# Stores begun by GpSimd, operand rows asked for two at a time, and loads moved in the plan of a fused attention and two-layer kernel

## The chip, the cores and the metric

One core of a Trainium2 chip runs the whole program. The metric is the device time of one execution in microseconds (us). The kernel before took 1796.57 us (median of 3 runs, 1793.56 to 1800.48).

## What is computed

```python
# q, k, v: (8, 8, 576, 64)   batch, heads, sequence, head size
q_s = softmax(q, axis=-1);  k_s = softmax(k, axis=2)          # 1e-9 added to each sum
kv  = einsum('bhsd,bhse->bhde', k_s, v)
x   = einsum('bhsd,bhde->bhse', q_s, kv) -> (4608, 512)
x   = (silu(x @ w_gate) * (x @ w_val)) @ w_out                # 512 -> 1536 -> 512, float64 weights
out = elu(x @ w_in) @ w_out2                                  # 512 -> 2048 -> 512, float64 weights
```

Every matrix product is made from three float32r matmuls of high and low parts (hi x hi, hi x lo, lo x hi), so each operand is split by a ScalarE copy (hi) and a VectorE subtraction (lo).

## The kernel before, in words

The 4608 rows are nine blocks of 512. The order of the work is written out by hand: every engine has its own queue in program order, and an instruction that must wait stops everything behind it on its engine. A DMA is such an instruction too, on the queue of the engine that begins it. SyncE (SP) begins nearly all of them, ScalarE the stores of converted weights and of partial outputs, GpSimd none.

**First stage** (`run_a`, about 28 to 550 us). For block i there are six f (128 of the first 768 hidden columns), each with sub-steps s = 0 (gate projection), 1 (value projection) and 2 (product with `w_out` for the f before). A sub-step written (f, s) below also carries attention work for block t = i + 1, named in `PLAN` (line 1778; `PLAN0` and `PLAN1` serve i = 0 and 1). For t >= 3 the normalised q is transposed through DRAM: `qturn` transposes on VectorE, `qout` (line 548) stores to `dq`, `qin` (line 555) loads pairs into two `qT` buffers, `xT` (line 596) multiplies them with kv. `in0` and `in1` are the two halves of `qin`; `xT0` uses in0's pairs and `xT2` in1's, so in1's load overwrites buffers that xT0's matmuls (line 638) read. `load_k`, `load_v` and `load_q` fetch the next block's inputs, `kmax` and `qmax` are their first readers on VectorE.

Alongside, `conv` (line 278) turns float64 weights into float32 in four steps: load, scale, bits, split. From weight chunk 21 on, the result goes to DRAM: single chunks by one store (line 244), pairs of chunks by `sums_out` (line 266), in which GpSimd makes four sums and ScalarE begins four stores two sub-steps later. Four `cd` buffers and one `st` buffer hold what is being stored. `store_x` (line 653) lets GpSimd add x's hi and lo parts; SP stores the rows two sub-steps later. `defer(age, fn)` puts fn off to a later call of `aged()`, and there is one such call for each sub-step or tick.

**Second stage** (`unit_b`, `single_b`, about 575 to 1009 us). The other 768 hidden columns, for units of two blocks, with products made from seven instead of eight sub-products (`product`, line 1093, with operands M1 to M7). Each step calls `tick` six times. A tick does at most one operation of `xd_tick` (line 1039), which prepares the operands of the last layer: `xd_rows` asks for rows of the block outputs `ys` (four loads, two tiles), `xd_open` makes the sums on GpSimd, and then in each tick one operand is split: a ScalarE copy into a fresh slot `xst` (line 1059) and, in the next tick, the VectorE subtraction (line 1033) and a store to `xd`. The slot goes back (`drop`) as the store is begun. `slot4` hands out the slot that has been vacant longest from one pool of 25, which `g` tiles, operands and weights share. In the first unit the weight sums `s` are split in place (`part_split`, line 1067) on ScalarE and VectorE.

**Third stage** (`run_2`, from about 1009 us): the last layer in the same manner. `load_s` (line 1338) loads a step's weight sums and puts their split in a list; `hold` counts the steps that it waits there, and `run_splits` emits it in the middle of a step. For the first two steps `load_s(0)` and `load_s(1)` are called in `single_b` (line 1721).

Of the kernel before, what the change touches and what calls it, by code (L numbers as in the profile page):

```python
# [17 lines left out]
def kernel(  # L18
# [103 lines left out]
    def drop(n):  # L122
        vacant.append(n)
# [103 lines left out]
    def conv_split(eng):  # L227
        n = stage["split"]
        if n >= stage["bits"]:
            return  # L230
        kind, f = chunks[n][0]
        if n >= NA1 and kind in "giv":
            if stage["bits"] < n + 2:
                return
            d1, d2 = ds[n].bitcast(FP32), ds[n + 1].bitcast(FP32)
            sums_out(sd[f // 2] if kind == "i" else sf[kind, (f - HALF) // 2], d1, d2)
            stage["split"] += 2
            ds.pop(n)
            ds.pop(n + 1)
            return  # L240
        if n >= NA1:
            stage["split"] += 1
            d = ds.pop(n).bitcast(FP32)
            defer(1, lambda: nc.scalar.dma_start(out=wd[f] if kind == "p" else wb[f], in_=d))
            return
        if not room(("w",)):
            return
        at, w = slot4(("w",), [128, 2, 512], "w")
        stage["split"] += 1
        df = ds.pop(n).bitcast(FP32)  # L250
        nc.scalar.activation(out=w[:, 0, :], in_=df, func=ACTF.Copy)
        eng.tensor_tensor(w[:, 1, :], df, w[:, 0, :].bitcast(FP32), op=ALU.subtract)  # L252
        W[chunks[n][0]] = w
        wslot[chunks[n][0]] = at
# [11 lines left out]
    def sums_out(dst, d1, d2):  # L266
        st = sums(d1, d2)
        flat = lambda t: t.rearrange("p a n -> p (a n)")

        def store():  # L270
            nc.scalar.dma_start(out=dst[0][:, 0], in_=d1[:, 0:256])
            nc.scalar.dma_start(out=flat(dst[1][:, 0:2]), in_=d2)
            nc.scalar.dma_start(out=flat(dst[0][:, 1:4]), in_=flat(st[:, 0:3]))
            nc.scalar.dma_start(out=dst[1][:, 2], in_=st[:, 3])

        defer(2, store)

# [375 lines left out]
    def store_x(t, n):  # L653
        if n == 0:
            x32[t] = ev_p.tile([128, KD, TB], FP32, tag="ev", name="ev")
        x, ns = x_t["a", t], slice(2 * n, 2 * n + 2)
        for c in range(2 * n, 2 * n + 2):
            nc.gpsimd.tensor_tensor(
                x32[t][:, c], x[:, c, 0, :].bitcast(FP32), x[:, c, 1, :].bitcast(FP32),
                op=ALU.add,  # L660
            )
        defer(2, lambda: nc.sync.dma_start(out=xs[t][:, ns], in_=x32[t][:, ns]))

    def first_block():
        kt = at1.tile([128, H, 4, D], FP32, tag="k", name="k")
# [201 lines left out]
    def emit_B(ph, i, f):  # L867
        if f == 0:
            acc_tiles((ph, i))
        at, gt = G.pop((ph, i, f))  # L870
        w = W["o", f]
        last = f == HALF - 1
        for c in range(KD):
            cs = slice(c * 128, (c + 1) * 128)
            mm3(acc[ph, i][c], (w[:, 0, cs], w[:, 1, cs]), (gt[:, 0, :], gt[:, 1, :]),
                f == 0, last)
        drop(at)
        if i == NB - 1:
            drop(wslot.pop(("o", f)))
        if last:  # L880
            ev = ev_p.tile([128, KD, TB], FP32, tag="ev", name="ev")
            for c in range(KD):
                nc.scalar.activation(out=ev[:, c, :], in_=acc[ph, i][c], func=ACTF.Copy)
            nc.scalar.dma_start(out=yps[i], in_=ev)


    yp_t = {}
# [111 lines left out]

    def xd_rows(k):  # L1000
        m, c = divmod(k, 2)
        tags, r = [], []
        for n in range(2):
            at, t = slot4(ANY, [128, 2, TB], "yr", FP32)
            tags.append(at)
            for e in range(2):
                nc.sync.dma_start(out=t[:, e], in_=ys[2 * m + e][:, c + 2 * n])
                r.append(t[:, e])
        xd_r[k] = [0, tags, r]

    def xd_open(k):
        m, c = divmod(k, 2)
# [16 lines left out]
    def xd_lo():  # L1029
        if xd_st["lo"]:  # L1030
            op, src, at, d = xd_st["lo"]
            m, c = xd_st["cur"][0:2]
            nc.vector.tensor_tensor(d[:, 1, :], src, d[:, 0, :].bitcast(FP32), op=ALU.subtract)
            defer(1, lambda: (
                nc.sync.dma_start(out=xd[m][PROD[op]][:, c], in_=d.bitcast(FP32)), drop(at)
            ))
            xd_st["lo"] = None

    def xd_tick(ready):
        k, n = xd_st["k"], xd_st["rows"]  # L1040
        for e in xd_r.values():
            e[0] += 1
        if n < min(6, 2 * ready, k + 2) and room(ANY) >= (4 if n == k else 8):
            xd_rows(n)
            xd_st["rows"] += 1
        if xd_st["cur"] is None:
            if k not in xd_r or xd_r[k][0] < 5:
                return
            xd_open(k)
        xd_lo()  # L1050
        ops = xd_st["cur"][3]
        if not ops:
            for at in xd_st["cur"][2]:
                drop(at)
            xd_st.update(cur=None, k=k + 1)
            return
        op, src, pre = ops.pop(0)
        at, d = slot4(ANY, [128, 2, TB], "xst")
        nc.scalar.activation(out=d[:, 0, :], in_=src, func=ACTF.Copy)
        pre()  # L1060
        xd_st["lo"] = (op, src, at, d)
# [2 lines left out]

    splits, split_now = [], []

    def part_split(hi, lo, age=0):
        nc.scalar.activation(out=hi, in_=lo.bitcast(FP32), func=ACTF.Copy)
        defer(age, lambda: nc.vector.tensor_tensor(  # L1069
            lo, lo.bitcast(FP32), hi.bitcast(FP32), op=ALU.subtract  # L1070
        ))

# [337 lines left out]
    def load_sb(key, parts=(0, 1), n=None, first=False):  # L1410
        for part in parts:
            at = n
            if n is None:
                at = ring[part] % 2
                ring[part] += 1
            t = s_tile(at, part)
            SW.setdefault(key, [None, None])[part] = t
            if not first:
                nc.sync.dma_start(out=t.bitcast(FP32), in_=sb[key][part])
                continue  # L1420
            nc.sync.dma_start(out=t[:, :, 1, :].bitcast(FP32), in_=sf[key][part])
            splits.append([0, lambda age, t=t, part=part: (
                part_split(t[:, :, 0, :], t[:, :, 1, :], age),
                defer(2, lambda: nc.sync.dma_start(out=sb[key][part], in_=t.bitcast(FP32))),
            )])

# [273 lines left out]
    def single_b(u, carry):  # L1700
        NG1 = HALF // 2
        nxt = units[0]
        for g in range(NG1):
            if g == 0:
                mid = carry
                for key in (("g", 1), ("v", 1)):
                    load_sb(key, n=2 if key[0] == "g" else 3)
            else:
                mid = [lambda f=HALF + 2 * g - 2 + e: b_D(u[0], f) for e in range(2)]
            if g == 1:  # L1710
                load_yp(u[0])
            if g == 1:
                x_small(nxt, X_MID[0:2], ANY)
            step_s(u, g, mid, lambda: (aged(), xd_st["k"] < 6 and xd_tick(3)), g == NG1 - 1)
            if g == 0:
                load_sb(("g", 2), n=0)
                load_sb(("v", 2), n=1)
                X[nxt] = ({}, [])
                x_big(nxt, X_HEAD)
            if g == 1:  # L1720
                load_s(0)
                load_s(1)
                x_small(nxt, X_MID[2:], ANY)
        while xd_st["k"] < 6 or later:
            aged()
            if xd_st["k"] < 6:
                xd_tick(3)
        for tag in X.pop(u)[1]:
            drop(tag)
        x_big(nxt, X_LAST)  # L1730
        for f in range(4):
            load_p(f, hold=1 + f // 2)
        carry = [lambda f=f: b_D(u[0], f) for f in (F1 - 2, F1 - 1)]
        carry.append(lambda: (load_s(2), load_s(3, 1), None)[2])
        return carry
# [12 lines left out]
    def side_last(ff, s):  # L1748
# [36 lines left out]
    }  # L1785
    PLAN0 = {
# [15 lines left out]
    def steps(i):  # L1802
# [3 lines left out]
        if t < B:  # L1806
# [7 lines left out]
            else:  # L1814
                st["kturnt"] = lambda: kturn(t)
                st["ks0"] = lambda: ks(t, (0, 1), nc.vector)
                st["ks1"] = lambda: (ks(t, (2, 3, 4), nc.vector), u < B and load_k(u))
            st["load_v"] = lambda: load_v(t)
            if i == 0:
                st["load_k2"] = lambda: load_k(u)  # L1820
# [208 lines left out]
```

## Time and profile before

| | |
|---|---|
| median of 3 runs | 1796.57 us |
| profiled execution: its own time, its span | 1795.31 us, 1793.2 us |
| TensorE matmuls busy | 1682.0 us (94%) |
| VectorE / ScalarE / GpSimd busy | 66% / 45% / 13% |
| granted TensorE clock, mean | 0.976 of full speed |
| DMA moved | 351.95 MB, mean 196 GB/s |

PE stands for TensorE's matmuls, DVE for VectorE, ACT for ScalarE, POOL for GpSimd, SPq and ACTq for the DMA instructions on an engine's queue. A busy PE is not PE at its peak: the time that counts is where it stands still, and the stretch after that in which its clock is granted at half. What ended the chain of work is 73% PE, 9% DMA, 8% DVE, 5% ACT.

### The profile page before, as it was taken

The numbers are of one execution on the slowest core, as the hardware profiler recorded it, in microseconds if no ns is written. First come the engines' busy times: TensorE is split into PE (matmuls) and PEld (weight loads), VectorE is DVE, ScalarE is ACT, GpSimd is POOL, SyncE is SP. The second block draws the span as 40 slices with busy tenths as digits, with TensorE's granted clock in tenths as the row PEclk, the third lists the DMA queues.
The fourth block names the chain that finished last, engine by engine and source line by source line (L and its number), as shares of the span: only waits on it lengthen the run. The fifth ranks groups of instructions, "written<-read, shape, count | busy, mean of one in ns | idle before, by whom it ended". The sixth has DMA issues, their size and how long they took to land.

```text
span 1793.2 us, 22155 instructions
## 1 busy us (share of the span) xinstructions
PE 1682.0 (94%) x8228; PEld 1375.0 (77%) x8228; DVE 1186.3 (66%) x1800; ACT 801.8 (45%) x1339; POOL 233.8 (13%) x196
## 2 busy tenths in 40 slices
PE   6899998889998999998989689999999999999999
PEld 4577777667877788787878568888889888888887
DVE  7858787677756766666756376657674767465574
ACT  4645244334433432323323265656464656355453
POOL 3611121222104204032120000000000000000000
PEclk9999998899999999999999899999999999999999
DMA  9475876695675757587686926272613453352511
GB/s 283 114 181 162 244 231 217 197 267 196 207 246 220 248 221 268 213 302 272 238 304 254 400 71 242 76 270 94 246 67 113 142 198 115 143 184 75 211 47 71
DMA packets 186860, 351.95 MB, mean 196 GB/s; under 512 B 49921, under 2 KB 121857, under 8 KB 172801
## 3 DMA queue, kind: packets, MB, share of 16 engines
q1 hardware_dynamic: 174224, 322.49, 53.2%
q10 hardware_dynamic: 12528, 28.05, 4.2%
q8 instruction: 64, 1.05, 0.2%
q14 instruction: 44, 0.35, 0.1%
HBM read 234.36 MB, written 116.14 MB: 195 GB/s over the span
## 4 chain that ended last, share of the span: by engine, by line
PE 73%; DMA 9%; DVE 8%; ACT 5%; issue 2%; SPq 2%; POOL 2%; ACTq 0%; DVEq 0%; POOLq 0%
PE p L1104 27%; PE y L810 11%; PE y L809 10%; PE y L808 10%; PE a L827 4%; PE a L828 4%; PE a L831 4%; DMA xd<-xst 2%; DVE u L1228 1%; DMA qT<-dq 1%; PE t L638 1%; ACT th L1117 1%; ACT e L1118 1%; DMA s<-sd 1%; PE t L480 1%
## 5 line engine op out<-in xcount | busy, mean ns | idle before, releaser
L1104 PE MATMUL p<-xp,s 128*128 128x512 f32 x1344 | 325.4, 396 | 37.2 <-DVE u L1228 20.4
L1228 DVE TENSOR_TENSOR u<-u,p 128x512 f32<-128x512 f32 x315 | 215.7, 685 | 218.0 <-PE p L1104 203.5
L1104 PEld LDWEIGHTS p<-xp,s 128*128 128x128 f32 x1344 | 255.6, 191 | 94.8 <-DVE u L1228 24.2
L1104 PE MATMUL p<-xs,s 128*128 128x512 f32 (+1 forms) x1260 | 274.4, 372 | 3.1 <-ACT u L1248 3.1
L1104 PEld LDWEIGHTS p<-xs,s 128*128 128x128 f32 x1260 | 224.1, 191 | 45.0 <-ACT u L1248 3.7
L809 PE MATMUL y<-w,g 128*128 128x512 f32 x576 | 225.7, 392 | 4.2 <-DVE w L1069 4.2
L808 PE MATMUL y<-w,g 128*128 128x512 f32 x576 | 225.4, 391 | 1.7 <-ACT g L1143 1.3
L810 PE MATMUL y<-w,g 128*128 128x512 f32 x576 | 226.0, 392 | 0.6
L827 PE MATMUL a<-x,w 128*128 128x512 f32 x424 | 171.1, 403 | 4.5 <-DVE th L858 2.7
L828 PE MATMUL a<-x,w 128*128 128x512 f32 x424 | 167.6, 395 | 0.0
L1123 DVE SCALAR_TENSOR_TENSOR th<-e,th 128x512 f32<-128x512 f32 x144 | 99.2, 689 | 101.9 <-ACT e L1118 100.5
L1116 ACT ACTIVATE e<-u 128x512 f32<-128x512 f32 x108 | 67.7, 627 | 156.3 <-DVE u L1228 156.3
L809 PEld LDWEIGHTS y<-w,g 128*128 128x128 f32 x576 | 108.8, 189 | 27.4 <-DVE w L1069 4.9
L810 PEld LDWEIGHTS y<-w,g 128*128 128x128 f32 x576 | 108.8, 189 | 26.5 <-DVE g L1152 4.0
L808 PEld LDWEIGHTS y<-w,g 128*128 128x128 f32 x576 | 108.9, 189 | 24.8 <-ACT g L1143 1.7
L1152 DVE TENSOR_TENSOR g<-th,g 128x512 fp32r<-128x512 f32 (+1 forms) x160 | 99.9, 634 | 37.7 <-ACT g L1143 35.3
L1143 ACT ACTIVATE g<-th 128x512 fp32r<-128x512 f32 (+1 forms) x160 | 91.3, 580 | 67.7 <-DVE th L1129 67.7
L831 PE MATMUL a<-x,w 128*128 128x512 f32 x424 | 114.4, 392 | 0.6 <-POOL w L252 0.6
L827 PEld LDWEIGHTS a<-x,w 128*128 128x128 f32 x424 | 81.1, 191 | 29.9 <-issue 7.5
L831 PEld LDWEIGHTS a<-x,w 128*128 128x128 f32 x424 | 80.1, 189 | 17.9 <-POOL w L252 1.1
L828 PEld LDWEIGHTS a<-x,w 128*128 128x128 f32 x424 | 81.2, 191 | 16.3
L1117 ACT ACTIVATE th<-e 128x512 f32<-128x512 f32 x144 | 91.1, 633 | 4.6
(204 smaller groups left out, 2638.8 us busy)
## 6 DMA issues: line engine op xcount, KB each, us to landing
xp<-xd SPq DMA_DIRECT2D x32, 1024.0 KB, 10.1
xs<-xd SPq DMA_DIRECT2D x51, 512.0 KB, 7.2
xd<-xst SPq DMA_DIRECT2D x42, 512.0 KB, 9.4
raw<-in_moe_w_out SPq DMA_DIRECT2D x26, 512.0 KB, 5.0
s<-sbg SPq DMA_DIRECT2D x12, 1024.0 KB, 6.5
s<-sbv SPq DMA_DIRECT2D x12, 1024.0 KB, 8.8
yp<-ev ACTq DMA_DIRECT2D x9, 1024.0 KB, 4.5
xs<-ev SPq DMA_DIRECT2D x18, 512.0 KB, 5.1
```

The lines of the kernel that those rows point to most:

```text
L808: nc.tensor.matmul(out=ps, lhsT=wh, rhs=xh, start=first, stop=False)
L809: nc.tensor.matmul(out=ps, lhsT=wh, rhs=xl, start=False, stop=False)
L810: nc.tensor.matmul(out=ps, lhsT=wl, rhs=xh, start=False, stop=last)
L827: nc.tensor.matmul(out=ps, lhsT=wh, rhs=x[:, c, 0, :], start=(c == 0), stop=False)
L828: nc.tensor.matmul(out=ps, lhsT=wh, rhs=x[:, c, 1, :], start=False, stop=False)
L831: nc.tensor.matmul(out=ps, lhsT=wl, rhs=x[:, c, 0, :], start=False, stop=(c == KD - 1))
L1104: nc.tensor.matmul(out=out_, lhsT=w, rhs=x, start=first and (q, c, k) == (0, 0, 0), stop=(c, k) == (1, 2), skip_group_check=True,)
L1117: nc.scalar.activation(out=t, in_=e, func=ACTF.Tanh, scale=-0.5)
L1123: nc.vector.scalar_tensor_tensor(out=t, in0=e, scalar=1.0, in1=t, op0=ALU.add, op1=ALU.mult)
L1143: nc.scalar.activation(out=gt[:, 0, at:at + n], in_=t[:, q * n:(q + 1) * n], func=ACTF.Copy)
L1152: nc.vector.tensor_tensor(gt[:, 1, at:at + n], t[:, q * n:(q + 1) * n], gt[:, 0, at:at + n].bitcast(FP32), op=ALU.subtract,)
L1228: nc.vector.tensor_tensor(o, a, b, op=ALU.add)
```

## The change

Six edits. (1) The stores of converted weights, of their sums and of x's rows are begun by GpSimd; x's rows without the delay of two sub-steps. (2) The store of the partial output `yps` is begun by SP at the next `aged()` instead of by ScalarE. (3) `xd_rows` asks for one tile (two loads) in a tick, and a set opens four ticks after its second tile; an `xst` slot goes back two ticks after its store is begun, and no operand is started while fewer than three slots are vacant. (4) Part 0 of the first unit's weight sums is subtracted by GpSimd. (5) The split of the last layer's second step waits one step more. (6) In `PLAN`, in1 goes from (4, 0) to (3, 2), load_q from (3, 0) to (4, 0), load_k from (1, 0) to (2, 0), kspread from (4, 2) to (5, 1), qmax0 from (4, 2) to (5, 1).

```diff
@@ conv_split
-            defer(1, lambda: nc.scalar.dma_start(out=wd[f] if kind == "p" else wb[f], in_=d))
+            defer(1, lambda: nc.gpsimd.dma_start(out=wd[f] if kind == "p" else wb[f], in_=d))
@@ sums_out, store()
-            nc.scalar.dma_start(out=dst[0][:, 0], in_=d1[:, 0:256])
...
+            nc.gpsimd.dma_start(out=dst[0][:, 0], in_=d1[:, 0:256])
+            nc.gpsimd.dma_start(out=flat(dst[1][:, 0:2]), in_=d2)
+            nc.gpsimd.dma_start(out=flat(dst[0][:, 1:4]), in_=flat(st[:, 0:3]))
+            nc.gpsimd.dma_start(out=dst[1][:, 2], in_=st[:, 3])
@@ store_x
-        defer(2, lambda: nc.sync.dma_start(out=xs[t][:, ns], in_=x32[t][:, ns]))
+        nc.gpsimd.dma_start(out=xs[t][:, ns], in_=x32[t][:, ns])
@@ emit_B
-            nc.scalar.dma_start(out=yps[i], in_=ev)
+            defer(0, lambda: nc.sync.dma_start(out=yps[i], in_=ev))
@@ xd_rows
-        tags, r = [], []
-        for n in range(2):
-            at, t = slot4(ANY, [128, 2, TB], "yr", FP32)
-            tags.append(at)
-            for e in range(2):
-                nc.sync.dma_start(out=t[:, e], in_=ys[2 * m + e][:, c + 2 * n])
-                r.append(t[:, e])
+        tags, r = xd_r.get(k, (0, [], []))[1:]
+        n = len(tags)
+        at, t = slot4(ANY, [128, 2, TB], "yr", FP32)
+        tags.append(at)
+        for e in range(2):
+            nc.sync.dma_start(out=t[:, e], in_=ys[2 * m + e][:, c + 2 * n])
+            r.append(t[:, e])
         xd_r[k] = [0, tags, r]
+        return n == 1
@@ xd_lo
-                nc.sync.dma_start(out=xd[m][PROD[op]][:, c], in_=d.bitcast(FP32)), drop(at)
+                nc.sync.dma_start(out=xd[m][PROD[op]][:, c], in_=d.bitcast(FP32)),
+                defer(2, lambda: drop(at)),
@@ xd_tick
-            xd_rows(n)
-            xd_st["rows"] += 1
+            xd_st["rows"] += xd_rows(n)
...
-            if k not in xd_r or xd_r[k][0] < 5:
+            if k not in xd_r or len(xd_r[k][1]) < 2 or xd_r[k][0] < 4:
                 return
...
+        if room(ANY) < 3:
+            return
         op, src, pre = ops.pop(0)
@@ part_split, load_sb
-    def part_split(hi, lo, age=0):
+    def part_split(hi, lo, age=0, eng=None):
...
-                part_split(t[:, :, 0, :], t[:, :, 1, :], age),
+                part_split(t[:, :, 0, :], t[:, :, 1, :], age, nc.vector if part else nc.gpsimd),
@@ single_b
-                load_s(1)
+                load_s(1, 1)
@@ PLAN, steps
-        "in0": (2, 1), "load_q": (3, 0), "in1": (4, 0), "kspread": (4, 2),
-        "xT0": (3, 2), "xT1": (3, 2), "kturn": (4, 0), "xT2": (5, 0), "xT3": (5, 0),
-        "qmax0": (4, 2), "qmax1": (5, 2),
+        "in0": (2, 1), "load_k": (2, 0), "load_q": (4, 0), "kspread": (5, 1),
+        "xT0": (3, 2), "xT1": (3, 2), "in1": (3, 2), "kturn": (4, 0), "xT2": (5, 0), "xT3": (5, 0),
+        "qmax0": (5, 1), "qmax1": (5, 2),
...
-                st["ks1"] = lambda: (ks(t, (2, 3, 4), nc.vector), u < B and load_k(u))
+                st["ks1"] = lambda: ks(t, (2, 3, 4), nc.vector)
+                if u < B:
+                    st["load_k"] = lambda: load_k(u)
```

## Rows read from the trace of the kernel before

**Rows 1.** The page's first part: busy us (share of the span) x instructions.
```profile
PE 1682.0 (94%) x8228; PEld 1375.0 (77%) x8228; DVE 1186.3 (66%) x1800; ACT 801.8 (45%) x1339; POOL 233.8 (13%) x196
```
**Rows 2.** Waits of PE, whole span: us in total, times, longest us.
```profile
PE t L638 <- DMA qT<-dq: 29.3, 4, 9.4
PE p L1104 <- DVE u L1228: 20.4, 7, 5.7
PE p L1104 <- DVE s L1069: 10.3, 1, 10.3
...
PE p L1104 <- ACT s L1068: 6.4, 1, 6.4
```
**Rows 3.** Waits of PE between 700 and 930 us, same columns.
```profile
PE p L1104 <- DVE u L1228: 14.4, 3, 5.7
```
**Rows 4.** Timeline of PE at stalls: start us, duration us, work, [idle before <- releaser].
```profile
275.00 0.66 PE L638 MATMUL t<-qT,bd 64*64 64x256 f32 x1 [8.34 <-DMA qT<-dq]
...
405.38 0.87 PE L638 MATMUL t<-qT,bd 64*64 64x384 f32 x1 [9.44 <-DMA qT<-dq]
...
822.78 1.65 PE L1104 MATMUL p<-xp,s 128*128 128x512 f32 x3 [5.71 <-DVE u L1228]
...
1026.79 4.18 PE L1104 MATMUL p<-xp,s 128*128 128x512 f32 x10 [10.30 <-DVE s L1069]
```
**Rows 5.** Windows behind two stalls: stretch, length, busy by engine, granted clock, DMA.
```profile
275.00:279.40 4.40, 4.40 (x21) 2.85 (x22) 1.23 (x2) 1.08 (x2) 2.24 (x4) 0.51 0.49 153
822.80:828.90 6.10, 6.10 (x14) 4.77 (x15) 3.26 (x5) 1.64 (x3) 0.00 (x0) 0.50 0.87 357
```
**Rows 6.** Timeline of SP's DMA issues in one block of the first stage.
```profile
232.01 0.37 SPq L340 DMA_DIRECT2D k<-in_k  x1
...
245.63 0.82 SPq L558 DMA_DIRECT2D qT<-dq  x2
...
246.97 7.90 SPq L352 DMA_DIRECT2D vtile<-in_v  x5
...
256.14 2.13 SPq L550 DMA_DIRECT2D dq<-qn  x4
259.58 6.28 SPq L367 DMA_DIRECT2D q<-in_q  x4
265.90 2.49 SPq L377 DMA_DIRECT2D q<-in_q  x4
...
269.43 1.02 SPq L558 DMA_DIRECT2D qT<-dq  x2
```
**Rows 7.** Timeline of SP two blocks later.
```profile
386.75 2.84 SPq L550 DMA_DIRECT2D dq<-qn  x4
```
**Rows 8.** Tile view of `dq`: stores to it and loads from it together.
```profile
DMA to landing us min/median/max: 2.6/3.9/7.2
```
**Rows 9.** Tile view of `qT`: its loads alone.
```profile
DMA to landing us min/median/max: 2.6/3.4/6.1
```
**Rows 10.** Window of one block: length, busy PE, PEld, DVE, ACT, POOL, clock, DMA.
```profile
238.22:303.10 64.88, 56.54 (x330) 45.20 (x332) 47.95 (x75) 26.72 (x37) 11.18 (x12) 0.92 0.74 229
```
**Rows 11.** Timeline of ACT at the second and third stage's stalls.
```profile
820.77 1.15 ACT L1059 ACTIVATE xst<-yr 128x512 fp32r<-128x512 f32 x2 [4.68 <-DMA xd<-xst]
...
1014.16 1.97 ACT L1068 ACTIVATE s<-s 128x1024 fp32r<-128x1024 f32 x2 [17.01 <-DMA s<-sd]
1016.79 1.96 ACT L1068 ACTIVATE s<-s 128x1024 fp32r<-128x1024 f32 x2 [0.66 <-DMA s<-sd]
```
**Rows 12.** Timeline of POOL and DVE in the first unit of the second stage.
```profile
595.60 13.67 POOL L1370 TENSOR_TENSOR v<-v 128x512 f32<-128x512 f32 x8 [31.31 <-DMA v<-xs]
...
595.17 3.18 DVE L1069 TENSOR_TENSOR s<-s 128x1024 fp32r<-128x1024 f32 x2
598.27 1.78 DVE L1469 TENSOR_TENSOR th<-th,u 128x512 f32<-128x512 f32 x1
599.97 0.67 DVE L1469 TENSOR_TENSOR th<-th,p 128x512 f32<-128x512 f32 x1
```

More of the change, by code (lines that the diff above doesn't have):

```diff
@@ L270, in store @@
         def store():
-            nc.scalar.dma_start(out=dst[0][:, 0], in_=d1[:, 0:256])
-            nc.scalar.dma_start(out=flat(dst[1][:, 0:2]), in_=d2)
-            nc.scalar.dma_start(out=flat(dst[0][:, 1:4]), in_=flat(st[:, 0:3]))
-            nc.scalar.dma_start(out=dst[1][:, 2], in_=st[:, 3])
+            nc.gpsimd.dma_start(out=dst[0][:, 0], in_=d1[:, 0:256])
+            nc.gpsimd.dma_start(out=flat(dst[1][:, 0:2]), in_=d2)
+            nc.gpsimd.dma_start(out=flat(dst[0][:, 1:4]), in_=flat(st[:, 0:3]))
+            nc.gpsimd.dma_start(out=dst[1][:, 2], in_=st[:, 3])
         defer(2, store)
@@ L1065 @@
     splits, split_now = [], []
-    def part_split(hi, lo, age=0):
+    def part_split(hi, lo, age=0, eng=None):
         nc.scalar.activation(out=hi, in_=lo.bitcast(FP32), func=ACTF.Copy)
-        defer(age, lambda: nc.vector.tensor_tensor(
+        defer(age, lambda: (eng or nc.vector).tensor_tensor(
             lo, lo.bitcast(FP32), hi.bitcast(FP32), op=ALU.subtract
```

## The prediction, written before the changed kernel was run

> **What bounds the kernel now.** I read the busy shares first: TensorE works 94% of the span [rows 1], so only what is left of it, and stretches at half clock, can be won. The view that decides is therefore the list of TensorE's waits [rows 2]. It has four waits for `qT<-dq`, 29.3 us together, in the first stage; waits for VectorE's line 1228, of which three with 14.4 us lie in the second stage [rows 3]; and two at the start of the last layer, 6.4 and 10.3 us, for the splits of the weight sums `s`. The timeline then shows each of them as one gap [rows 4], and the windows behind a gap show a second price: the granted clock is 0.51 for 4.4 us after the first-stage gap at 275 us and 0.50 for 6.1 us after the one at 822.8 us [rows 5]. That is the lower of the two levels (1.2 of 2.4 GHz), it falls while TensorE stands idle, and work at half speed costs 2.2 and 3.0 us in these two places. The rest of the span has no gap of this size that the diff touches, so I cost the change gap by gap.
>
> **The change, part by part.** The sum is made against the profiled execution, 1795.31 us (span 1793.2), which lies 1.3 us below the median of the runs, 1796.57.
>
> *First-stage loads (edit 6).* Today SP begins, in order, v (246.97 to 254.87), the `dq` stores of the second half (256.14 to 258.27), load_q (259.58 to 268.39, so 6.28 + 2.49 us of issue), and only then in1 at 269.43 [rows 6]. TensorE stands from 275.00 - 8.34 = 266.66 on [rows 4]. So it is the queue order and not the data that makes in1 late. With the new plan in1 stands ahead of load_q. It can't start before the `dq` stores have landed: 258.27 + 3.9 (median, [rows 8]) = 262.2; and it lands 3.4 us later [rows 9], at 265.6. Needed: 266.66. In the block of the longest gap the stores are issued by 386.75 + 2.84 = 389.59 [rows 7]; plus 7.3 makes 396.9, against 405.38 - 9.44 = 395.94 needed, so about 1 us of the gap stays. Moving load_k from (1, 0) to (2, 0) works against this: its 1.1 MB, asked for at 232.01 today [rows 6], would go out at about 242, between the first `dq` stores and in0. SP has free time there (it waits for the `dq` landing until 245.63), so the issue is covered; its bytes at the block's mean of 229 GB/s [rows 10] are 5 us of transfer. They push v and the `dq` stores back by between 0 (the same bytes leave the stretch just ahead, so the backlog there is shorter) and 5 us. I take 1 us, near the first end, because the queue stands idle for lack of data there. Behind in1, load_q is the one that is late next: 8.77 us of issue from about 262 to 271, and qmax0 moves to (5, 1), which VectorE reaches near 270. It waits 1 to 3 us there and the value projection's product waits behind it; TensorE needs that product's bank only two sub-steps later, so I cost 0 to 1.5 us per block and take 0.7. The whole budget is 29.3 us of gaps and 4 x 2.2 us of half clock, 38 us (the clock price of one gap taken for all four). What stays: about 1 + 1 us late landing in two blocks and 4 x 0.7, together 5. **Gain 33 us**, bounds 10 (k's 5 us and a `dq` landing at its maximum of 7.2 us hit every block) and 38.
>
> *Room for the faster step.* A block takes 64.88 us with 8.34 + 2.2 of it lost, so about 54 us without, and VectorE is busy for 47.95 us of it [rows 10]: 6 us of slack are left, which matters for the first rival.
>
> *Stores begun by GpSimd, and `yps` by SP (edits 1, 2).* No row shows a DMA that GpSimd begins. Per block there are about 12 to 14 such stores from `conv` (a pair of chunks gives 4, a single one 1) and 2 of x's rows, so 15. Bounds for one: nothing for anybody else, or, if GpSimd's work for it disturbs VectorE as its arithmetic does, the whole lost time of such a meeting, 1.78 - 0.67 = 1.1 us of VectorE [rows 12]. GpSimd itself is busy for 11.18 of 64.88 us [rows 10], so even at 1.3 us each (20 us) it has the time. I take the value near nothing, since the nearest thing of the same kind, SP's DMA issues at 0.4 us apiece [rows 6], hides in the 6 us of slack (15 x 0.4). ScalarE loses these issues, which gains nothing, as it is busy for 26.72 us of a block [rows 10]. The queue that these stores are moved behind is GpSimd's own, where `store_x` waits for the `yps` landing; stores queued behind it hold `cd` buffers longer, and the one place where VectorE would feel that is the end of the conversion, near 540 us, by 0 to 4 us. There the subtraction of two part-0 sums leaves VectorE as well (edit 4). I set this against that and count 0.
>
> *Operand slots (edit 3).* At 820.77 ScalarE has waited 4.68 us to write a slot whose store has not left yet [rows 11]; VectorE's subtraction and the additions of line 1228 stand behind it, and TensorE loses 5.71 us [rows 4] and 3.0 us of clock [rows 5]. The slot had been handed back when its store was begun. Returned two ticks later and with three slots kept vacant, the next user gets one that has been still for longer; with too few slots it skips the tick instead of stopping ScalarE. Three such gaps are 14.4 us [rows 3], with clock 14.4 + 3 x 3.0 = 23. What is late next: the operations skipped fall into later ticks, at worst into the closing loop of `single_b`, and the wait for the rows themselves remains. **Gain 19 us**, bounds 5 and 23.
>
> *Second step's split (edit 5).* ScalarE waits for the sums of the first step until 1014.16 and goes on with those of the second, 0.66 + 1.96 us until 1018.75, with the last step's gate work and the first split's subtraction behind it [rows 11]; TensorE's 10.30 us end with that [rows 4]. Holding the second split takes 2.6 us off this chain. It comes back inside the next step, where it may delay something by up to 2 us. **Gain 2.5 us**, bounds 0 and 4.
>
> *Subtraction on GpSimd (edit 4).* Near 600 us VectorE's two subtractions take 3.18 us beside GpSimd's sums [rows 12], and one of them goes. **Gain 1.5 us**, bounds -2 (GpSimd's sums, and so the contention, last longer) and 2.
>
> Sum: 33 + 19 + 2.5 + 1.5 = 56 us. 1795.3 - 56 = 1739, on the median's scale 1740.6; with half of the small later prices that I set to nothing I say **1742 us**. Its own range, from the bounds of the two large terms: 1728 to 1762.
>
> **The rivals.**
> (a) *VectorE pays for GpSimd's DMAs* (slower). If each of the 15 stores of a block costs VectorE c us, a block can't be shorter than 47.95 + 15c. Up to c = 0.4 nothing happens; at c = 1.1 the first stage gains nothing; from about c = 1.5 the loss in four blocks (15 x 0.4 x 4 = 24) outweighs edits 3 to 5 (23). At c = 1.78, a whole contended operation, a block takes 74.7 us, 4 x 9.8 = 39 more, less 23: 1812 us. For it: VectorE's operations do stretch beside GpSimd's arithmetic [rows 12]. Against: beginning a DMA is not arithmetic on 512 columns.
> The Trainium skill ("SBUF — State Buffer", section "Who interferes with whom") says that a VectorE instruction with two SBUF inputs contends with a GpSimd instruction that reads SBUF and not with one that only writes, and infers that making DMA descriptors needs the writing side. The first half agrees with the 1.78 against 0.67 us; no run so far shows the second. By that rule c is near nothing and the forecast stands; it is one reason why I give this rival little.
> (b) *in1 is still late.* k's bytes and the `dq` landing push it back by 4 to 5 us in each block, so half of the first stage's 33 us stays: 1742 + 17 = 1759. For: the second block worked out above already misses by 1 us. Against: load_q's 8.77 us of issue certainly leave the way.
> (c) *The operand waits move instead of going* (the pool of 25 runs short, rows or `g` tiles wait in turn): 19 us stay, 1761. For: stores begun late share the same transfers.
> (d) *Both (b) and (c)*: 1742 + 17 + 19 = 1778.
> (e) *Nothing changes that can be measured*, because the gaps close into others as long: 1790 to 1797.
>
> **How the numbers follow.** Forecast 0.54, (a) 0.10, (b) 0.15, (c) 0.09, (d) 0.05, (e) 0.07. Differences under 0.5% (9 us) are about what a measurement of this kernel can't tell from no change. Faster by more than that: 0.54 + 0.15 + 0.09 + 0.05 = 0.83; within: 0.07; slower: 0.10. For the range I leave out the slower case and most of (e) above, and let the low end reach to both large gains at their upper bounds with a few us of the rest: 1724 to 1788.
>
> **What would show it.** In the trace after, the four waits of line 638 for `qT<-dq` are gone or under 2 us each, in1's issue stands ahead of load_q's, and a block of the first stage takes 54 to 56 us. The three waits of line 1228 between 700 and 930 us are gone, ScalarE's line 1059 no longer waits for `xd<-xst`, and no window behind them shows the clock at 0.5. At the start of the last layer ScalarE goes from the first pair of line 1068 straight to the gate work. The prediction is wrong if VectorE's mean for lines 212 to 219 or 858 rises well above the 0.67 us of an undisturbed operation [rows 12] in the first stage, if its waits for `q<-in_q` grow beyond the two sub-steps and TensorE waits for line 858, or if the operands pile up behind the last step of `single_b`.

## The result, and the profile after

The changed kernel takes **1766.16 us** (median of 1762.41 to 1769.02), against 1796.28 in the same runs: ratio 0.9829, 95% interval 0.98 to 0.9858. That is 30 us faster; the forecast was 54 us faster (1742, own range 1728 to 1762, wide range 1724 to 1788). The direction held and the size did not. The profiled execution took 1764.12 us, its span is 1762.4. Of all executions reported here one, of `k_early`, took 4188.05 us; it is in no ratio and in no median below.

First the page's busy shares of the changed kernel, to be read against [rows 1]:

```profile
PE 1679.9 (95%) x8228; PEld 1371.1 (78%) x8228; DVE 1188.9 (67%) x1794; ACT 799.4 (45%) x1339; POOL 299.7 (17%) x298
```

GpSimd has 102 instructions and 66 us more: a DMA that it begins stands in the profile as an instruction. VectorE has as much work as before. Next TensorE's waits over the whole span of the changed kernel, columns as in [rows 2]:

```profile
PE p L1107 <- DVE u L1231: 9.5, 6, 3.7
PE y L809 <- DVE g L846: 9.2, 4, 4.7
...
PE p L1107 <- DVE s L1072: 7.7, 1, 7.7
PE t L638 <- DMA qT<-dq: 6.4, 5, 2.5
PE p L1107 <- ACT s L1071: 5.7, 1, 5.7
PE c L638 <- DVE cd L219: 4.6, 4, 1.4
```

The three waits that the change was costed by have shrunk: `qT<-dq` from 29.3 to 6.4 us, line 1228 (now 1231) from 20.4 to 9.5, line 1069 (now 1072) from 10.3 to 7.7. Beside them the wait for line 846 has grown, from 5.1 us before, and that for line 219 is new; both lines are VectorE's. The windows (columns as in [rows 5]) say where the gain came in. Between the first products of line 480 (`vtile` by `ke`) in the fourth and the last of the eight blocks that have them, before:

```profile
177.60:433.10 255.50, 226.15 (x1314) 180.81 (x1314) 194.07 (x295) 100.95 (x141) 61.11 (x61) 0.93 0.74 225
```

and after:

```profile
177.90:419.50 241.60, 228.47 (x1313) 179.72 (x1312) 196.12 (x290) 99.77 (x140) 92.77 (x118) 0.97 0.83 240
```

These four blocks, for which the forecast had 33 us, gained 13.9; one takes 60.4 us in the mean, where 54 to 56 was forecast. TensorE's idle time in them fell by 16.2 us (29.4 to 13.1) and its busy time rose by 2.3. What the clock costs there (busy time times the share of the clock that was not granted, summed over windows of 1 us) is 6.4 us, against 8.3 before: of the 8.8 us that the budget had for it, about 2 came back. From there to the second stage's first product it lost 2.7 (142.8 to 145.5); the second stage's units up to the first `xa` product gained 16.2 (386.0 to 369.8); the rest gained 3.7 (831.3 to 827.6). The timeline of TensorE after the change, at its stalls:

```profile
254.31 0.61 PE L638 MATMUL t<-qT,bd 64*64 64x256 f32 x2 [1.44 <-DMA qT<-dq]
256.30 0.68 PE L638 MATMUL c<-qT,bd 64*64 64x256 f32 x1 [1.38 <-DVE cd L219]
...
328.70 0.72 PE L638 MATMUL t<-qT,bd 64*64 64x320 f32 x2 [0.88 <-DMA qT<-dq]
...
391.74 0.50 PE L638 MATMUL t<-qT,bd 64*64 64x384 f32 x1 [2.50 <-DMA qT<-dq]
...
560.12 0.80 PE L809 MATMUL y<-g,w 128*128 128x512 f32 x1 [4.73 <-DVE g L846]
...
870.78 1.66 PE L1107 MATMUL p<-xp,s 128*128 128x512 f32 x6 [2.27 <-DVE u L1231]
...
996.32 2.07 PE L1107 MATMUL p<-xp,s 128*128 128x512 f32 x4 [7.68 <-DVE s L1072]
```

The stall at 996.32 answers to that of 10.30 us in [rows 4]. The one at 870.78 is one of two that are left between 700 and 930 us (the other, of 1.93 us, stands before 776.86); neither is at the place of one of the three before. In the block that had the 8.34 us there are now two gaps of 1.4, and the clock is paid again: the window right behind them shows 0.50, the lower of the two levels, as in [rows 5].

```profile
258.00:262.00 4.00, 4.00 (x12) 3.02 (x10) 3.66 (x6) 1.36 (x3) 4.00 (x7) 0.50 1.06 274
```

Why a gap is left, SP's timeline of that block tells (compare [rows 6]):

```profile
238.32 3.20 SPq L550 DMA_DIRECT2D dq<-qn  x4
241.57 0.47 SPq L340 DMA_DIRECT2D k<-in_k  x1
...
246.76 1.33 SPq L558 DMA_DIRECT2D qT<-dq  x2
...
258.06 2.23 SPq L550 DMA_DIRECT2D dq<-qn  x4
...
264.09 1.16 SPq L558 DMA_DIRECT2D qT<-dq  x2
...
265.81 1.90 SPq L367 DMA_DIRECT2D q<-in_q  x4
```

in1 is ahead of load_q, as planned. The late load of this block is now **in0**, asked for at 246.76 and needed at 254.31 - 1.44 = 252.87, and k has been put just in front of it. In the two blocks behind it in1 is late as well, at 328.70 and 330.61 and at 391.74. Of the 6.4 us in the list, in0 has 2.3 and in1 4.2. k's own landing has grown, by the issue view (KB, median us to landing; 178 to 410 us), and VectorE waits for it at `kmax0`, where it did not wait before; for load_q it waits 8.4 us in three blocks at `qmax0` (1 to 3 us a block were forecast), less than the 16.7 us of before:

```profile
k<-in_k SPq DMA_DIRECT2D x4, 1024.0 KB, 11.5
```

```profile
DVE km L389 <- DMA k<-in_k: 8.6, 4, 3.6
DVE qr L503 <- DMA q<-in_q: 8.4, 3, 3.2
```

### The profile page after: what moved, and what is told of

It is laid out like the page before. It is cut to its first block, busy times and chain, and to the rows that moved or that the text cites. A ratio compares the mean times of both kernels' runs of the same rounds, so it can differ in the third digit from the quotient of the medians.

```text
span 1762.4 us, 22232 instructions
## 1 busy us (share of the span) xinstructions
PE 1679.9 (95%) x8228; PEld 1371.1 (78%) x8228; DVE 1188.9 (67%) x1794; ACT 799.4 (45%) x1339; POOL 299.7 (17%) x298
## 4 chain that ended last, share of the span: by engine, by line
PE 67%; DVE 13%; DMA 8%; ACT 6%; issue 3%; SPq 2%; POOL 2%; DVEq 0%; ACTq 0%; POOLq 0%
PE p L1107 27%; PE y L810 10%; PE y L809 10%; PE y L808 10%; PE a L827 3%; PE a L831 3%; PE a L828 3%; DMA k<-in_k 2%; DVE u L1231 2%; DMA q<-in_q 1%; ACT th L1120 1%; ACT e L1121 1%; DMA s<-sd 1%; ACT e L1119 1%; DMA xs<-xd 1%
## 5 line engine op out<-in xcount | busy, mean ns | idle before, releaser
L1107 PE MATMUL p<-xp,s 128*128 128x512 f32 x1344 | 321.6, 393 | 22.8 <-DVE u L1231 9.5
L827 PEld LDWEIGHTS a<-x,w 128*128 128x128 f32 x424 | 80.7, 190 | 30.5 <-issue 6.2
L840 ACT ACTIVATE g<-th 128x512 fp32r<-128x512 f32 x54 | 33.9, 628 | 153.9 <-DVE th L858 153.9
L809 PE MATMUL y<-g,w 128*128 128x512 f32 x216 | 86.1, 399 | 9.2 <-DVE g L846 9.2
L831 PEld LDWEIGHTS a<-x,w 128*128 128x128 f32 x424 | 79.9, 189 | 17.9 <-POOL w L252 1.0
## 6 DMA issues: line engine op xcount, KB each, us to landing
xp<-xd SPq DMA_DIRECT2D x32, 1024.0 KB, 10.3
```

The lines of the kernel that those rows point to most:

```text
L809: nc.tensor.matmul(out=ps, lhsT=wh, rhs=xl, start=False, stop=False)
L827: nc.tensor.matmul(out=ps, lhsT=wh, rhs=x[:, c, 0, :], start=(c == 0), stop=False)
L831: nc.tensor.matmul(out=ps, lhsT=wl, rhs=x[:, c, 0, :], start=False, stop=(c == KD - 1))
L1107: nc.tensor.matmul(out=out_, lhsT=w, rhs=x, start=first and (q, c, k) == (0, 0, 0), stop=(c, k) == (1, 2), skip_group_check=True,)
```

## Experiments

Two theories at the start. **K**: moving load_k to (2, 0) eats the gain. **G**: the DMAs that GpSimd begins slow VectorE. What the texts on record call "the sixth value projection", and the table "sixth", is the last of the products of line 480 above, at 433.1 us before. All runs in one table; ratio to the kernel before with its interval; "k" is the median landing of load_k between 178 and 410 us; the last two columns are when the sixth product of line 480 and the second stage start, each in one profiled execution. Up to the sixth product the changed kernel and `no_gp_sub` are the same program and differ by 4 us there, so I read no smaller difference of that column.

| kernel | ratio | interval | median us | k us | sixth | 2nd stage |
|---|---|---|---|---|---|---|
| before | 1 | | 1797 | 6.7 | 433.1 | 575.9 |
| changed | 0.9829 | 0.98-0.9858 | 1766.2 | 11.5 | 419.5 | 565.0 |
| plan_only | 0.9852 | 0.9837-0.9867 | 1770.3 | 6.9 | 410.2 | 551.3 |
| slots_only | 0.9906 | 0.9892-0.9919 | 1781.0 | 6.6 | 435.2 | 577.3 |
| no_gp_sub | 0.9814 | 0.9793-0.9835 | 1763.8 | 11.6 | 415.4 | 561.2 |
| scalar_stores | 0.9798 | 0.977-0.9826 | 1760.4 | 10.8 | 417.5 | 562.1 |
| x_on_sp | 0.9797 | 0.977-0.9823 | 1759.0 | 8.4 | 415.7 | 559.0 |
| no_gp_dma | 0.979 | 0.9771-0.9809 | 1760.2 | 8.4 | 412.9 | 558.0 |
| yps_scalar | 0.9817 | 0.9798-0.9837 | 1764.9 | 11.3 | 421.0 | 567.6 |
| k_early | 0.9753 | 0.9739-0.9766 | 1753.7 | 6.1 | 405.5 | 551.3 |
| k_early_scalar | 0.9763 | 0.9741-0.9785 | 1754.1 | 6.6 | 408.3 | 553.8 |
| k_early_no_gp_dma | 0.9789 | 0.9761-0.9816 | 1758.4 | 6.4 | 411.7 | 555.5 |
| k_early_no_gp_sub | 0.9749 | 0.9729-0.9768 | 1753.1 | 5.5 | 404.0 | 548.9 |
| k_early_stores_back | 0.9753 | 0.9729-0.9777 | 1752.5 | 6.6 | 408.4 | 550.8 |

**The plan alone.** The kernel before, with edit 6 and nothing else (the new `PLAN`, and `load_k` as a step at (2, 0)).

> The kernel before with the new plan of the loads alone (edit 6); stores, operand slots, split and subtraction as before. Theory K (moving load_k to (2, 0) eats part of the gain: k's bytes go out ahead of in0 and kmax0 waits for them): the first stage is shorter by about 14 us up to the sixth value projection, as in the changed kernel, VectorE waits for k<-in_k for 7 to 9 us in all, and the time is 1796 - 14 = 1782 (1779 to 1786). Rival G (GpSimd's DMAs slow VectorE, and the plan alone is worth what was forecast): without them the plan gains 25 to 33 us, 1763 to 1771.

Measured 26.6 us (23.9 to 29.3). That is in theory G's range, and theory K as put fell: with the other edits left out the same move of k costs VectorE 0.9 us of waits. k lands in 6.9 us here (issue view, 178 to 410 us):

```profile
k<-in_k SPq DMA_DIRECT2D x4, 1024.0 KB, 6.9
```

**The operand slots alone.** The kernel before with the new `xd_rows`, `xd_lo` and `xd_tick` (edit 3).

> The kernel before with the operand slots alone (edit 3). Forecast: 19 us, 1777. From the two traces (the second stage's units gained about 16 us): 1780 (1778 to 1783), with TensorE's gaps at 724, 822 and 920 us under 2.5 us each. If the gain in the units came from stores that the other edits put elsewhere: 1788 or more.

Measured 16.9 us (14.6 to 19.4). Its waits of TensorE keep those of the first stage and of the third stage's start, and of the three between 700 and 930 us [rows 3] 4.6 us are left (second fence: 640 to 960 us):

```profile
PE t L638 <- DMA qT<-dq: 29.8, 4, 9.5
PE p L1107 <- DVE s L1072: 10.3, 1, 10.3
```

```profile
PE p L1107 <- DVE u L1231: 4.6, 3, 2.3
```

The 10.3 us stay in every run without edit 5 and are 7.7 to 8.0 in every run with it, so the held split is worth about 2.6 us of that stall; no run has edit 5 alone.

**k back.**

```
-        "in0": (2, 1), "load_k": (2, 0), "load_q": (4, 0), "kspread": (5, 1),
+        "in0": (2, 1), "load_k": (1, 0), "load_q": (4, 0), "kspread": (5, 1),
```

> The changed kernel with load_k back at (1, 0), behind ks1, and the rest of the new plan kept. Theory K: VectorE's 8.6 us of waits for k<-in_k go, in0 lands in time for xT0 (gaps of 1.44, 0.88 and 0.84 us go), and with the half clock behind them the first stage is 6 to 10 us shorter: 1756 to 1760. Rival G: the gaps come from VectorE beside GpSimd's DMAs and stay: 1764 to 1768. Third way: k's bytes land where v's and the dq stores go out before, in1 is late again as in the kernel before, and the time rises to 1770 or more.

44.4 us (42.0 to 46.9), so 0.0076 of 1797 or some 14 us better than the changed kernel, with intervals apart. That is 2 us below theory K's range, and theory G's 1764 to 1768 fell. TensorE has no wait for `qT<-dq` left in the first stage and VectorE none for k. The window of the same four blocks:

```profile
177.80:405.50 227.70, 221.88 (x1315) 177.05 (x1314) 199.49 (x292) 99.48 (x140) 92.34 (x119) 0.99 0.83 251
```

So k's move is the loss in the changed kernel and almost free in `plan_only`: its price depends on the other edits. I call this theory S: the move is dear only beside the stores that GpSimd begins.

**The subtraction back on VectorE (edit 4 undone).**

```
-                part_split(t[:, :, 0, :], t[:, :, 1, :], age, nc.vector if part else nc.gpsimd),
+                part_split(t[:, :, 0, :], t[:, :, 1, :], age),
```

> The changed kernel with the subtraction of the part-0 sums back on VectorE (edit 4 undone). Theory (the subtraction on GpSimd holds VectorE up at the second stage's start: 5.20 us for an operation beside it, a gap of 4.73 us): the first product of the second stage comes 2 to 3 us earlier after the end of the first stage, and the time is 1762 to 1764. Rival (the start is held by GpSimd's chain of stores and sums, whoever subtracts): the gap stays, 1765 to 1768. As forecast, edit 4 a gain of 1.5 us: 1767 to 1769.

In the changed kernel GpSimd subtracts from 553.62 on, and two VectorE subtractions beside it take 5.20 us; they are followed by the 4.73 us gap (first GpSimd's, then VectorE's timeline):

```profile
553.62 4.68 POOL L1072 TENSOR_TENSOR s<-s 128x1024 fp32r<-128x1024 f32 x2
```

```profile
554.27 5.20 DVE L1407 TENSOR_TENSOR xs<-v,xs 128x512 fp32r<-128x512 f32 x2 [2.17 <-ACT xs L1406]
```

With the edit undone the same two take 1.29 us and that gap is gone, but its neighbours grow (VectorE's row, then TensorE's; the gaps at 552.15 and 592.82 were 1.61 and 3.72 us):

```profile
554.93 1.29 DVE L1407 TENSOR_TENSOR xs<-v,xs 128x512 fp32r<-128x512 f32 x2 [2.16 <-ACT xs L1406]
```

```profile
552.83 0.79 PE L827 MATMUL a<-x,w 128*128 128x512 f32 x1 [3.91 <-DVE th L858]
...
590.01 2.93 PE L1107 MATMUL p<-xp,s 128*128 128x512 f32 x6 [5.28 <-DVE u L1231]
```

The stretch from the sixth product to the second stage is 145.8 us without the edit and 145.5 with it. The place was named rightly and the net is nothing that these runs can tell.

**Who begins the stores.** `scalar_stores`: converted weights and sums back on ScalarE. `x_on_sp`: x's rows back on SP, two ticks late. `no_gp_dma`: both. `yps_scalar`: `yps` back on ScalarE. Each from the changed kernel.

```
-            defer(1, lambda: nc.gpsimd.dma_start(out=wd[f] if kind == "p" else wb[f], in_=d))
+            defer(1, lambda: nc.scalar.dma_start(out=wd[f] if kind == "p" else wb[f], in_=d))
...
-        nc.gpsimd.dma_start(out=xs[t][:, ns], in_=x32[t][:, ns])
+        defer(2, lambda: nc.sync.dma_start(out=xs[t][:, ns], in_=x32[t][:, ns]))
...
-            defer(0, lambda: nc.sync.dma_start(out=yps[i], in_=ev))
+            nc.scalar.dma_start(out=yps[i], in_=ev)
```

> The changed kernel with the stores of converted weights and sums back on ScalarE (that part of edit 1 undone); x's rows stay on GpSimd, load_k at (2, 0). Theory S (k's move is dear only because GpSimd begins its stores in one bunch with it: k lands in 11.5 us in the changed kernel, in 6.9 us with the new plan alone): k lands in 7 to 8 us, the sixth value projection starts near 410 instead of 419.5, the second stage's first product comes 142 us after that instead of 145.5, and the time is 1750 to 1756. Rival K (k's move costs the same whoever stores): 1764 to 1768.

> The changed kernel with the stores of x's rows back on SP, two ticks late (that part of edit 1 undone); converted weights and sums stay on GpSimd. If the bunch of theory S is made by the two 512-KB stores of x's rows: k lands in about 8 us and the time is 1753 to 1758. If it is made by the converted weights behind store_x on GpSimd: k lands in 10 us or more and the time stays at 1763 to 1768.

> The changed kernel with no DMA begun by GpSimd (converted weights and sums on ScalarE, x's rows on SP two ticks late), load_k still at (2, 0), yps on SP. Theory B (each large store that goes out just ahead of the moved k load puts k later; the run with x's rows alone on SP had k at 8.9 us and 1759, the new plan alone 6.9): k lands in 7 us, the sixth value projection starts at 410 to 412 and the time is 1753 to 1757. Rival Y (the store of yps on SP's queue is the culprit): k lands in 9 to 11 us and the time is 1759 to 1764.

> The changed kernel with the store of yps back on ScalarE (edit 2 undone); the other stores on GpSimd, load_k at (2, 0). Theory B: its 1 MB leaves some 10 us before k in either queue, so nothing changes: k lands in 10 to 12 us, 1763 to 1768. Rival Y: k lands in 7 to 8 us, 1754 to 1758.

`scalar_stores` missed theory S: k still takes 10.8 us, the sixth product starts at 417.5. x's rows are the larger part: with them on SP k lands in 8.4 us, and VectorE's waits for k are gone (0.4 us in `no_gp_dma`), though the 1759.0 us are 1 us above the range expected. `no_gp_dma` missed too: k in 7 us and 1753 to 1757 were expected, and 8.4 and 1760.2 lie nearer to rival Y, the store of `yps` on SP. Beside GpSimd's stores `yps` on either queue changes nothing (11.3 us, 1764.9). Without them it stays open: up to the sixth product `no_gp_dma` differs from `plan_only` (6.9 us) in `yps` alone. What differs is seen beside k's issue. In `plan_only` the second half of x's rows leaves SP behind k:

```profile
240.61 0.39 SPq L340 DMA_DIRECT2D k<-in_k  x1
...
243.51 0.40 SPq L662 DMA_DIRECT2D xs<-ev  x1
```

So it does in all four blocks, by 2.9 to 7.2 us. In the changed kernel GpSimd does its stores in the order of its own work, here between 235 and 242 us, and those 512 KB and a 256 KB weight store leave within 1 us ahead of k's issue at 241.57:

```profile
235.05 0.56 POOL L662 DMA_DIRECT2D xs<-ev  x1 [0.41 <-POOL ev L658]
...
237.77 2.54 POOL L658 TENSOR_TENSOR ev<-x 128x512 f32<-128x512 f32 x2
240.72 0.55 POOL L662 DMA_DIRECT2D xs<-ev  x1 [0.41 <-POOL ev L658]
241.27 0.55 POOL L244 DMA_DIRECT2D wb<-cd  x1
```

In the other three blocks they do not leave ahead of k: the second half goes 1.7 to 2.5 us behind its issue, as in the next block (SP, then GpSimd):

```profile
298.66 1.66 SPq L340 DMA_DIRECT2D k<-in_k  x1
```

```profile
301.12 0.55 POOL L662 DMA_DIRECT2D xs<-ev  x1 [0.41 <-POOL ev L658]
301.67 0.54 POOL L244 DMA_DIRECT2D wb<-cd  x1
```

k lands in 10.7 to 12.8 us in all four blocks, so a place just ahead of k is not needed. While this k is under way (12.8 us) the DMA engines are about as full, and move no fewer bytes a second, as beside the same block's k in `plan_only` (6.5 us). The windows of the two, changed kernel first:

```profile
298.66:311.46 12.80, 12.80 (x85) 10.67 (x82) 9.10 (x16) 2.74 (x5) 6.41 (x9) 1.00 0.97 285
```

```profile
298.97:305.47 6.50, 6.50 (x30) 5.38 (x29) 6.33 (x13) 1.51 (x3) 0.00 (x0) 1.00 1.02 267
```

12.8 us at 285 GB/s are 3.6 MB, 6.5 us at 267 are 1.7 MB. The longer landing goes with twice the bytes moved in the meantime, not with slower transfers.

Down the seven rows with k at (2, 0) the sixth product starts the later the longer k is under way: 6.9 us and 410.2, 8.4 and 412.9 to 415.7, 10.8 to 11.6 and 415.4 to 421.0. The ratios of `scalar_stores`, `x_on_sp` and `yps_scalar` overlap with the changed kernel's, so none of these edits alone is shown to change the time; that of `no_gp_dma` (0.979, up to 0.9809) just reaches the changed kernel's (from 0.98).

**k back, with the stores varied.** Load_k at (1, 0) with, in turn, the converted weights on ScalarE, no DMA of GpSimd's, no GpSimd subtraction, and edits 1 and 2 undone as a whole (the lines are those above).

> The changed kernel with load_k at (1, 0) and the stores of converted weights and sums on ScalarE. Theory S: with k out of the way the first stage does not care who stores (405 us up to the sixth value projection, as with load_k at (1, 0) alone), and only the end of the conversion gains (142 instead of 145.8 us to the second stage): 1754 - 4 = 1750 (1747 to 1752). Rival G (GpSimd's DMAs slow VectorE throughout): the first stage too is shorter, below 400, and the time is under 1747. If ScalarE's issues cost it what GpSimd's cost elsewhere: 1754 or more.

> The changed kernel with load_k at (1, 0) and no DMA begun by GpSimd: converted weights and sums on ScalarE, x's rows on SP two ticks late. It holds the new plan without k's move, the operand slots, the held split and yps on SP. By the separate runs (new plan alone 27.6 us, k at (1, 0) another 5, slots 17, held split 2.4): 1797.9 - 52 = 1746. Theory S: 1746 to 1751, the same as with x's rows on GpSimd or up to 2 us better. If GpSimd is the better place for x's rows, since SP's queue carries the loads: 1752 to 1757.

> The changed kernel with load_k at (1, 0) and the part-0 subtractions on VectorE (edit 4 undone). With load_k at (1, 0) alone 1754; the subtraction on GpSimd cost a gap of 4.73 us at the second stage's start, but without it the gaps around it grew by as much. If the two runs add: 1754 - 2.3 = 1752 (1750 to 1753). If edit 4 is neutral: 1753 to 1755.

> The changed kernel with load_k at (1, 0) and edits 1 and 2 undone as a whole: converted weights, sums and yps begun by ScalarE, x's rows by SP. If edits 1 and 2 give nothing once k is out of the way: 1752 to 1756, as with load_k at (1, 0) alone. If the GpSimd stores are worth something in the end (SP's and ScalarE's queues freed): 1758 or more, as the run without GpSimd's DMAs already suggests (1758.4). If they cost: under 1750.

With no DMA of GpSimd's no difference shows by where k is: 0.979 at (2, 0), 0.9789 at (1, 0). With the intervals of both runs taken together, that is 0 us give or take 6, and the 14 us above are give or take 6 too. So it is shown that the move's price depends on the stores, and not by how much. And with k early neither edit 1 nor edit 2 is worth anything that these runs show: 0.9753 with them, 0.9753 without. In `k_early_scalar` the first stage and the end of the conversion (145.5 us, not 142) gained nothing. `k_early_no_gp_dma` missed: I expected 1746 to 1751 and it took 1758.4; its interval overlaps with the others', and why it should lie above `k_early_stores_back`, which differs in `yps` alone, stays open. `k_early_no_gp_sub` is the fastest ratio, 0.9749, and can't be told from `k_early`. Both beat the changed kernel.

## Why the prediction was half right

**First-stage loads: 33 us forecast, 13.9 gained; the failing step.** The step was "They push v and the `dq` stores back by between 0 (the same bytes leave the stretch just ahead, so the backlog there is shorter) and 5 us. I take 1 us", for k's bytes. The new order of in1 and load_q does what was worked out: `plan_only` gains 26.6 us of the 33, and `k_early` has no wait for in1 left. The push was of the kind that I named, and I took it too small. Counted from each block's first product of line 480 (234.3, 297.0, 357.9 us in the changed kernel; 234.0, 293.7, 349.9 in `k_early`, which differs in load_k alone), the second `dq` stores begin 2.7, 8.4 and 5.2 us later in the changed kernel than in `k_early`, and in1's load 3.4, 7.0 and 5.6 us later. SP in the middle one of these blocks, changed kernel, then `k_early`:

```profile
319.03 2.17 SPq L550 DMA_DIRECT2D dq<-qn  x4
...
324.97 0.84 SPq L558 DMA_DIRECT2D qT<-dq  x2
```

```profile
307.29 2.31 SPq L550 DMA_DIRECT2D dq<-qn  x4
...
314.69 0.82 SPq L558 DMA_DIRECT2D qT<-dq  x2
```

And I left out two things that stand closer. One is in0, queued right behind k: it lands in 7.6, 8.0 and 6.9 us in these blocks, where the median of all such loads is 3.8 in `k_early`. The other is k's own landing, for which `kmax0` waits three sub-steps after the load: with 11.5 us under way instead of 6.9, VectorE loses 8.6 us in four waits. Little of this second one reaches TensorE: its waits for `cd` are as long in `k_early` (4.8 us against 4.6), where VectorE does not wait for k. Undoing the move gives 14 us back, in this kernel. In the two traces 13.9 of them are in these four blocks: 7.3 us less idle time, 6.4 of it the waits for in0 and in1, and 6.6 us less busy time, of which the clock has 4.7 (6.4 to 1.7, reckoned as above).

**Stores by GpSimd: 0 forecast, and the sum hid a product.** With load_k early they are indeed worth 0. I costed edits 1 and 6 one by one, and their prices do not add: the stores decide what moves beside k, the move decides that it matters. Shown: the 14 us when load_k is put back; that the same move costs nothing measurable without GpSimd's DMAs; that k lands in 8.4 instead of 11.5 us when only x's rows go back to SP, their second half behind k. Only argued: that the bytes moved beside k make its landing long. The windows speak for it, but no run changes when these stores leave and not their queue. Where the rest of 8.4 against 6.9 us comes from stays open.

**Rival (a), VectorE paying for GpSimd's DMAs, fell.** A DMA takes GpSimd 0.54 to 0.57 us (0.74 at most). VectorE's line 526 (two operands in SBUF) ran at its plain 1.23 us while GpSimd began three of them (GpSimd, then VectorE, changed kernel):

```profile
426.67 0.54 POOL L272 DMA_DIRECT2D sd<-cd  x1
427.19 0.54 POOL L273 DMA_DIRECT2D sd<-st  x1
427.73 0.54 POOL L274 DMA_DIRECT2D sd<-st  x1
```

```profile
427.15 1.23 DVE L526 TENSOR_TENSOR q<-q,qr 128x1024 f32<-128x1024 f32 x1
```

Between 110 and 560 us line 846 takes 0.68 us in the mean, both in 34 cases beside nothing and in 7 beside a DMA of GpSimd's, and 1.40 in 7 cases beside GpSimd's arithmetic (2.79 at most). The Trainium skill ("SBUF — State Buffer", section "Who interferes with whom") has this as a VectorE instruction with two SBUF inputs against a GpSimd instruction that reads SBUF, and infers that making descriptors needs the other side; the rows agree with both halves, though none shows what making a descriptor needs. What edit 1 does is to split `store_x`'s arithmetic, 6.64 us in one piece before, into two pieces with stores between them, and the second piece held line 846 for 2.74 us at 238.13. That is no bound: in `k_early` line 846 loses more (889 ns in the mean, 178 to 405 us, against 779 in the changed kernel) and it is 14 us faster.

**Operand slots: 19 forecast, 16.2 in the trace, 16.9 alone.** The gaps went from 14.4 to 4.2 us in two, not to 0; one of 2.27 us stands before 870.78. Line 1062 no longer waits for `xd<-xst`.

**Held split: 2.5 forecast, about 2.6 of the stall.** The rest of the third stage's 3.7 us is not pinned down.

**Subtraction on GpSimd: +1.5 forecast, about 0.** I looked at the meeting near 600 us and not at the one at 553.62, where it costs 4.73 us in one place and saves about as much around it.

**Rivals.** Nearest in mechanism was (b), k's bytes and the `dq` landing making in1 late (1759): in1 has 4.2 of the 6.4 us left, and in0, which it did not name, has the rest. The forecast's own range, 1728 to 1762, does not follow from the bounds of the two large terms: 38 and 23 give 1733, 10 and 5 give 1779. The measured time is outside the one and inside the other, and inside the range on record because that reaches to 1788 for the rivals. By terms: 13.9 - 2.7 + 16.2 + 3.7 = 31.1, within 0.3 us of the spans' difference of 30.8 (the two ends of the first stage, 177.6 and 177.9, make it up). Each of these is one execution of either kernel; `no_gp_sub`, the same program up to the sixth product, was 4 us faster there.

## What to carry to other kernels

When a load is moved, cost first who waits for that load itself, for the one queued next behind it and for what stands further down the same queue, and look which large stores leave in the microseconds around its new place, on every queue. Two edits that use the same stretch of the DMA engines are costed together, with one line for the pair, because each can be free alone. And a stall that is cut into two of 1.4 us need not have given its clock back: here it had not.

## What the runs showed of the hardware that was not expected

- A DMA begun by GpSimd occupies it for 0.54 to 0.57 us (0.74 at most) and stands in its busy time; x's rows cost it 0.55 us each (median of 18), where SP's issue of the same stores takes 0.36. Beside such an issue VectorE was not slowed (line 846: 0.68 us with and without).
- Two gaps of 1.4 us within 2 us were followed by a window at clock 0.50, the same level as behind the gap of 8.34 us [rows 5]. The size of a gap alone did not decide it: in `k_early` one of 1.69 us before 254.34 was followed by 2.5 us at 0.50, and in `plan_only` one of 1.73 us before 265.45 by a window at full clock:

```profile
265.40:269.40 4.00, 3.95 (x26) 2.68 (x27) 1.29 (x2) 1.09 (x2) 1.11 (x2) 1.00 0.97 355
```

- One and the same 1 MB load took 6.9 or 11.5 us (medians), with the same bytes to be moved in the block but in another order; the DMA engines moved 235 to 267 GB/s while it was under way in the first case and 275 to 286 in the second.
